# Where the range checks of the inputs run, and which product opens a group of eleven

## The chip, the cores and the metric

The kernel runs on one core of one Trainium2 chip. The metric is the device time of one execution in microseconds, the median of several runs. One execution was also recorded by the hardware profiler; its rows are what is read below. TensorE (PE in the rows, PEld its weight loads), VectorE (DVE), ScalarE (ACT), GpSimd (POOL) and SyncE (SP, which issues most transfers) each work through a queue of their own.

## What is computed

Three layers, one after the other, all in 32-bit floats. The first is a gated linear recurrence over 768 positions, for 2 x 8 heads of width 48; its output, 1536 tokens of 384 features, goes through a feed-forward layer 384 -> 2048 -> 384 with softplus, and that through a mix of four experts 384 -> 1024 -> 384 with relu, weighted by normalised probabilities.

```python
# q, k, v, a_re, a_im: (2, 8, 768, 48); (a_re, a_im) scaled to a length of at most 0.999 first
for t in range(S):
    S_re, S_im = ar * S_re - ai * S_im + k_t v_t^T, ar * S_im + ai * S_re
    y[:, :, t] = q_t @ S_re
x = y.transpose(0, 2, 1, 3).reshape(1536, 384)

h = x @ w_in                                            # 2048 wide
x = (np.maximum(h, 0) + np.log1p(np.exp(-np.abs(h)))) @ w_out

p = domain_probs / (domain_probs.sum(-1, keepdims=True) + 1e-09)
out = sum(p[:, e:e + 1] * (np.maximum(x @ w1[e], 0) @ w2[e]) for e in range(4))   # w1[e] 1024 wide
```

## The kernel before

**Numbers.** Each 32-bit operand is split into a high and a low part (two tiles of one buffer, index 0 and 1), and a product is three matmuls, high by high, low by high and high by low, into the same PSUM tile. A matmul is 128 x 128 weights by 384 columns unless said otherwise.

**Stages.** After the recurrence come twelve stages, run in the order k = 0, 1, 2, 3, 6, 7, 4, 5, 8, 9, 10, 11. k0 and k1 are the two halves of the softplus layer for batch 0, k6 and k7 those for batch 1; k2 to k5 are the four experts for batch 0, k8 to k11 for batch 1. The recurrence of batch 1 is spread over k2 and k3. `base` is the list of the stages' first steps: stage number m of that order begins at `base[m]`, and each has 16 steps (k0 has 24), so `base[3]` is k3, `base[8]` is k8 and `base[12]` the end of k11.

**Plain stages** (k0 to k3, k6, k7): a step is nine matmuls for a first-layer tile `h` (L232, PSUM tag "h", two buffers), the nonlinearity, and, `LAG` = 3 steps later, nine matmuls of the second layer into `y` and `z` (L319). In softplus the nonlinearity is Abs on ScalarE (L247, reads `h`), Exp and Ln on ScalarE (both in L103), then max(h, 0) + that on VectorE (L250, the last reader of `h`), and a split into `g` (L285, L286) a step later.

**Groups of eleven** (the stages in `FAST`, k4, k5 and k8 to k11): two tiles of weights by two blocks of tokens by three slices of the contraction would be 12 products; a scheme of sums and differences makes them from 11, at the price of VectorE and ScalarE work on sums of weights (`sA`, L499, L480, L481) and differences of tokens (`XC`). A group (k, j) is written by `part` in four quarters q = 0 to 3; after each quarter comes the second layer of an earlier tile (nine matmuls). There are four groups to a stage and 24 in all. The group's PSUM tiles are `px` (tag "h", two buffers), `pc` and `pv` (tag "a", three buffers). Quarter 0 of before makes product 7 into `px`, 3 and 4 into `pc`, copies `pc` to `ha` (ScalarE, L437) and adds `px` (VectorE, L438); then product 9 into `pv`, whose value ScalarE copies to `he` (L441). Quarter 1 adds products 0 and 2 to `pv`, so its first matmul must wait until `he` has been copied; the sum is copied to `hb` (L448), product 8 goes onto `px`, and VectorE adds them (L450). Quarter 2 adds two products to `px` and VectorE adds `he` (L456). Quarter 3 adds the last two. Each of the four results is activated (relu into `g`, L425 on ScalarE, L426 on VectorE).

**Range checks.** The fast path holds for inputs within certain ranges. 32 weight checks, `look_w`, each load one 384 KB tile of `w_in` or `w_out` again (`chkw`, L905, issued by SP), take Abs twice on ScalarE into `chkv` (L906, L907) and a maximum on VectorE (L908, `wmax`). Six `look`s at the decays each load two tiles, `chkr` and `chki` (L892, L893), take one Abs on ScalarE (L894) and four operations on VectorE (L895 to L898). All their tiles come from a ring of four buffers with the tag "raw", which the weight loads (`rawA`, `rawB`) use as well. `verdict` (from L911) puts the results together in small VectorE operations, one matmul `fl` (L922) and the flag `bad` (L923). The flag is read at the end of the fast path; where it is set, a general path computes everything anew.

**What sets the order.** `put(units, lo, hi)` spreads pieces of work evenly over the steps from lo to hi; `run` writes everything out in the order of these positions, and a scheduler then orders each engine's queue.

Of the kernel before, what the change touches and what calls it, by code (L numbers as in the profile page):

```python
# [75 lines left out]
def fast_path(ctx: ExitStack, tc, bad, wsc, qkv, a_re, a_im, w_in, w_out, probs, w1, w2, out):  # L76
    nc = tc.nc
# [24 lines left out]
    def act(out_, in_, fn, **kw):  # L102
        i = nc.scalar.activation(out_, in_, fn, **kw)  # L103
        if fn in (AF.Exp, AF.Ln, AF.Sin, AF.Arctan):
# [10 lines left out]
                            base=0, channel_multiplier=-1)  # L115
# [44 lines left out]
    def weights(k, n, tile):  # L160
# [23 lines left out]
        if k >= 2:  # L184
            return [load, lambda: part(z["raw"], slice(0, 768))]
# [9 lines left out]
        def conv(h):  # L195
            sl = slice(h * HW, (h + 1) * HW)
            f = tmp.tile([P, HW], I32, tag="f", name=f"f{nm}_{h}", bufs=2)
            join(nc, f, z["raw"][h])
            part(f.bitcast(F32), sl)
            nc.sync.dma_start(wsc[s * 8 + n, :, sl], f.bitcast(F32))  # L200
# [166 lines left out]
    def halves(b, d, t, q):  # L367
        return XB[b][:, q, d, t * WM:(t + 1) * WM]
# [36 lines left out]
    grp = {}  # L405

    def part(k, j, q):
        b = k // 6
        raws, sums = W[k, 2 * j]

        def prod(ps, w, x, start=False, stop=False):
            lt, li = (raws, w) if w < 5 else (sums, w - 5)
            for n, (p, r) in enumerate(((0, 0), (1, 0), (0, 1))):
                rhs = XC[b][:, r, x, :] if isinstance(x, int) else halves(b, *x, r)
                nc.tensor.matmul(ps, lt[:, p, li, :], rhs, start=(start and n == 0), stop=(stop and n == 2),  # L415
                                 skip_group_check=True)

        def keep(nm):
            return late["u"].tile([P, WM], F32, tag="h", name=f"{nm}{k}_{j}", bufs=3)

        def activate(f, blk, h):
            nm = f"{k}_{blk}_{f}"
            pool = tmp if blk == 0 else late["g"]
            g = pool.tile([P, 2, WM], F32R, tag="g", name="g" + nm, bufs=GB)
            nc.scalar.activation(g[:, 0, :], h, AF.Relu)  # L425
            nc.vector.scalar_tensor_tensor(g[:, 1, :], h, 0.0, g[:, 0, :].bitcast(F32), ALU.max, ALU.subtract)  # L426
            g_t[k, blk, f] = g

        if q == 0:
            x = grp["x"] = psum.tile([P, 512], F32, tag="h", name=f"px{k}_{j}", bufs=2)[:, :WM]  # L430
            c = psum.tile([P, 512], F32, tag="a", name=f"pc{k}_{j}", bufs=3)[:, :WM]
            v = grp["v"] = psum.tile([P, 512], F32, tag="a", name=f"pv{k}_{j}", bufs=3)[:, :WM]
            prod(x, 7, (1, 0), True, True)
            prod(c, 3, 0, True)
            prod(c, 4, (2, 0), False, True)
            h = keep("ha")
            nc.scalar.copy(h, c)  # L437
            nc.vector.tensor_tensor(h, x, h, ALU.add)  # L438
            prod(v, 9, (0, 1), True, True)
            e = grp["e"] = keep("he")  # L440
            nc.scalar.copy(e, v)  # L441
            activate(2 * j + 1, 0, h)
        elif q == 1:
            x, v = grp["x"], grp["v"]
            prod(v, 0, 3)
            prod(v, 2, (2, 0), False, True)
            h = keep("hb")
            nc.scalar.copy(h, v)  # L448
            prod(x, 8, 2, False, True)
            nc.vector.tensor_tensor(h, x, h, ALU.add)  # L450
            activate(2 * j, 0, h)
        elif q == 2:
            x, e = grp["x"], grp["e"]
            prod(x, 2, (2, 1))
            prod(x, 1, 4, False, True)
            nc.vector.tensor_tensor(e, x, e, ALU.add)  # L456
            activate(2 * j, 1, e)
        else:
            x = grp["x"]
            prod(x, 5, (2, 1))  # L460
            prod(x, 6, 1, False, True)
            activate(2 * j + 1, 1, x)
# [287 lines left out]
    def put(units, lo, hi):  # L750
        for i, u in enumerate(units):
            events.append((lo + (hi - lo) * i / len(units), len(events), u))

    def run():
        for _, _, u in sorted(events, key=lambda e: e[:2]):
            u()
        events.clear()
# [32 lines left out]
    base = [0] + [24 + 16 * i for i in range(12)]  # L790
# [96 lines left out]
    def look(part):  # L887
        def run_():
            r, i = (tmp.tile([P, 768], F32, tag="raw", name=f"chk{nm}{part}", bufs=4) for nm in "ri")
            z = hold(f"chkz{part}")  # L890
            rows_ = slice(part * 2 * P, (part + 1) * 2 * P)
            nc.sync.dma_start(r, a_re[rows_, :].rearrange("(p c) j -> p (c j)", p=P))  # L892
            nc.sync.dma_start(i, a_im[rows_, :].rearrange("(p c) j -> p (c j)", p=P))  # L893
            nc.scalar.activation(z, i, AF.Abs)  # L894
            nc.vector.scalar_tensor_tensor(z, r, SLOPE_MAX - 0.01, z, ALU.mult, ALU.subtract)  # L895
            nc.vector.tensor_reduce(vals[:, 0, part:part + 1], r, AX.X, ALU.min)
            nc.vector.tensor_reduce(vals[:, 1, part:part + 1], r, AX.X, ALU.max)
            nc.vector.tensor_reduce(vals[:, 2, part:part + 1], z, AX.X, ALU.min)  # L898
        return run_

    def look_w(i):
        def run_():
            raw = tmp.tile([P, HW, 2], I32, tag="raw", name=f"chkw{i}", bufs=4)
            t = hold(f"chkv{i}")[:, :HW]
            nc.sync.dma_start(raw.rearrange("p a w -> p (a w)"), w_raw[i // 16][i % 16 // 2, i % 2])  # L905
            nc.scalar.activation(t, raw[:, :, 1], AF.Abs)  # L906
            nc.scalar.activation(t, t, AF.Abs, bias=b_mid)  # L907
            nc.vector.tensor_reduce(wmax[:, i:i + 1], t, AX.X, ALU.max)  # L908
        return run_
# [15 lines left out]
    checks = [look_w(i) for i in range(32)]  # L925
    for i in range(6):
        checks.insert(6 * i + 3, look(i))
    put(checks + [verdict], base[8] + 2, base[12] - 2)
    run()
    flush()  # L930

# [153 lines left out]
@with_exitstack  # L1085
def attention_moe_kernel(ctx: ExitStack, tc, qkv, a_re, a_im, w_in, w_out, probs, w1, w2, v, out):
    nc = tc.nc
    top = ctx.enter_context(tc.tile_pool(name="top", bufs=1))
    bad = top.tile([1, 1], I32, name="bad")
    wsc = nc.dram_tensor("moe1_weights", (16, P, 768), F32).ap()  # L1090
    fast_path(tc, bad, wsc, qkv, a_re, a_im, w_in, w_out, probs, w1, w2, out)
    xs = nc.dram_tensor("attention_out", (NTOK, HD), F32).ap()
    flag = nc.values_load(bad[0:1, 0:1], min_val=0, max_val=1)
    with tc.If(flag > 0):
        general_path(tc, xs, v, qkv, a_re, a_im, w_in, w_out, probs, w1, w2, out)
# [53 lines left out]
```

## Time and profile before

| | us |
|---|---|
| median of three runs | 737.11 (736.68 to 737.11) |
| the profiled execution, its own time | 738.36 |
| its span in the profile | 736.6 |
| TensorE matmuls busy | 702.5 |
| TensorE weight loads busy | 674.9 |
| VectorE busy | 586.4 |
| ScalarE busy | 487.4 |
| first matmul of k8, k9, k10, k11 | 527.57, 577.62, 627.22, 673.80 |
| first output transfer issued | 724.13 |

Times of rows are microseconds from the start of the span. The profiled execution is 1.25 us above the median, and 1.76 of its time lie outside its span. Matmuls are pipelined and their recorded ends are modelled, so a stage's price is better read from its length and its number of matmuls than from their busy time. A chain that ended last was not resolved in this profile.

### The profile page before, as it was taken

The numbers are of one execution on the slowest core, as the hardware profiler recorded it, in microseconds if no ns is written. First come the engines' busy times: TensorE is split into PE (matmuls) and PEld (weight loads), VectorE is DVE, ScalarE is ACT, GpSimd is POOL, SyncE is SP. The second block draws the span as 40 slices with busy tenths as digits, with TensorE's granted clock in tenths as the row PEclk, the third lists the DMA queues.
The fourth block names the chain that finished last, engine by engine and source line by source line (L and its number), as shares of the span: only waits on it lengthen the run. The fifth ranks groups of instructions, "written<-read, shape, count | busy, mean of one in ns | idle before, by whom it ended". The sixth has DMA issues, their size and how long they took to land.

```text
span 736.6 us, 13285 instructions
## 1 busy us (share of the span) xinstructions
PE 702.5 (95%) x5159; PEld 674.9 (92%) x5159; DVE 586.4 (80%) x1149; ACT 487.4 (66%) x898; POOL 32.3 (4%) x31
## 2 busy tenths in 40 slices
PE   2789999999999999999999999999999999999996
PEld 1468899999899999999999999999999999999996
DVE  6999999955875854548888779988778898998963
ACT  7887976888896856345686665555556567766640
POOL 1122010000111001000000000000000000000000
PEclk9699999999999999999999999999999999999998
DMA  7665666621211420121022120213445345455401
GB/s 268 195 191 179 201 203 192 224 77 44 86 45 59 122 80 2 59 86 44 23 86 65 43 87 21 87 44 109 119 157 155 127 151 172 150 172 152 162 31 69
DMA packets 36342, 83.56 MB, mean 113 GB/s; under 512 B 4528, under 2 KB 13232, under 8 KB 36272
## 3 DMA queue, kind: packets, MB, share of 16 engines
q1 hardware_dynamic: 36272, 82.64, 35.5%
q8 instruction: 42, 0.69, 0.4%
q14 instruction: 28, 0.23, 0.1%
HBM read 73.95 MB, written 8.65 MB: 112 GB/s over the span
## 4 chain that ended last, share of the span: by engine, by line


## 5 line engine op out<-in xcount | busy, mean ns | idle before, releaser
L232 PE MATMUL h<-X,A 128*128 128x384 f32 (+1 forms) x936 | 175.9, 329 | 2.3 <-ACT A L181 0.8
L232 PEld LDWEIGHTS h<-X,A 128*128 128x128 f32 x936 | 153.4, 188 | 5.6 <-issue 1.6
L319 PE MATMUL y<-B,g 128*128 128x384 f32 x744 | 150.2, 335 | 0.2 <-DVE acc L350 0.2
L319 PEld LDWEIGHTS y<-B,g 128*128 128x128 f32 x744 | 131.0, 188 | 0.7 <-issue 0.5
L319 PE MATMUL y<-g,B 128*128 128x384 f32 (+1 forms) x504 | 91.0, 315 | 0.3 <-ACT g L285 0.3
L319 PE MATMUL z<-B,g 128*128 128x384 f32 x372 | 84.7, 334 | 0.0
L319 PEld LDWEIGHTS y<-g,B 128*128 128x128 f32 x504 | 79.3, 189 | 2.0 <-ACT g L285 0.6
L319 PEld LDWEIGHTS z<-B,g 128*128 128x128 f32 x372 | 66.3, 188 | 0.0
L247 ACT ACTIVATE e<-h 128x384 f32<-128x384 f32 (+1 forms) x60 | 30.8, 512 | 37.1 <-PE h L232 36.0
L250 DVE SCALAR_TENSOR_TENSOR e<-h,e 128x384 f32<-128x384 f32 (+1 forms) x60 | 34.9, 581 | 20.6 <-ACT e L103 19.8
L255 DVE SCALAR_TENSOR_TENSOR g<-h,g 128x384 fp32r<-128x384 f32 x32 | 17.7, 555 | 28.1 <-ACT g L254 28.1
L103 ACT ACTIVATE e<-e,b_one 128x384 f32<-128x384 f32 (+1 forms) x60 | 38.2, 637 | 1.3
L103 ACT ACTIVATE e<-e 128x384 f32<-128x384 f32 (+1 forms) x60 | 32.8, 547 | 1.3
L415 PE MATMUL px<-X,sA 128*128 128x384 f32 x144 | 33.4, 340 | 0.0
L319 PE MATMUL z<-g,B 128*128 128x384 f32 x144 | 32.9, 335 | 0.0
L415 PE MATMUL px<-XC,sA 128*128 128x384 f32 x144 | 32.8, 336 | 0.0
L664 PE MATMUL tp<-ident,QK 128*96 128x128 f32 x192 | 27.2, 288 | 5.7 <-DVE QK L655 4.6
L664 PEld LDWEIGHTS tp<-ident,QK 128*96 128x96 f32 x192 | 22.2, 133 | 10.3 <-DVE QK L655 6.2
L254 ACT ACTIVATE g<-h 128x384 fp32r<-128x384 f32 x32 | 15.6, 488 | 21.3 <-PE h L232 21.1
L286 DVE TENSOR_TENSOR g<-e,g 128x384 fp32r<-128x384 f32 x48 | 26.6, 555 | 3.7 <-ACT g L285 2.9
L480 ACT CAST B<-rawB 128x768 fp32r<-128x768 f32 x24 | 20.0, 834 | 14.4 <-DMA rawB<-in_w_dram 7.3
L350 DVE SCALAR_TENSOR_TENSOR acc<-y,pr,acc 128x384 f32<-128x384 f32 x46 | 26.3, 612 | 1.7 <-PE y L319 1.7
(204 smaller groups left out, 1416.7 us busy)
## 6 DMA issues: line engine op xcount, KB each, us to landing
rawA<-in_w_dram SPq DMA_DIRECT2D x32, 384.0 KB, 3.0
rawB<-in_w_dram SPq DMA_DIRECT2D x32, 384.0 KB, 3.1
rawA<-in_w_in_dram SPq DMA_DIRECT2D x16, 384.0 KB, 3.5
rawB<-in_w_out_dram SPq DMA_DIRECT2D x16, 384.0 KB, 3.8
chkw<-in_w_in_dram SPq DMA_DIRECT2D x16, 384.0 KB, 3.2
chkw<-in_w_out_dram SPq DMA_DIRECT2D x16, 384.0 KB, 3.2
qk<-in_qkv_dram SPq DMA_DIRECT2D x12, 384.0 KB, 3.4
v<-in_qkv_dram SPq DMA_DIRECT2D x12, 256.0 KB, 2.9
```

The lines of the kernel that those rows point to most:

```text
L103: i = nc.scalar.activation(out_, in_, fn, **kw)
L232: nc.tensor.matmul(ps, wt[:, p, kk, o:o + P], XB[b][:, q, kk, tok], start=(n == 0), stop=(n == 3 * KT - 1))
L247: nc.scalar.activation(t, h, AF.Abs)
L250: nc.vector.scalar_tensor_tensor(t, h, 0.0, t, ALU.max, ALU.add)
L254: nc.scalar.activation(g[:, 0, :], h, AF.Relu)
L255: nc.vector.scalar_tensor_tensor(g[:, 1, :], h, 0.0, g[:, 0, :].bitcast(F32), ALU.max, ALU.subtract)
L286: nc.vector.tensor_tensor(g[:, 1, :], t, g[:, 0, :].bitcast(F32), ALU.subtract)
L319: mm = nc.tensor.matmul(ys[j], l_, r_, start=(opens and n == 0 and not mate), stop=(closes and n == 2), skip_group_check=k == 0)
L350: nc.vector.scalar_tensor_tensor(dst, ys[j], pcol, dst, ALU.mult, ALU.add)
L415: nc.tensor.matmul(ps, lt[:, p, li, :], rhs, start=(start and n == 0), stop=(stop and n == 2), skip_group_check=True)
L480: nc.scalar.copy(hi, src)
L664: nc.tensor.transpose(tp[:96, hh, :], src[:, hf * 4 + hh, :], ident)
```

## The change

The 38 checks keep their sequence and are spread over the steps from `base[3] + 2` (in k3) to `base[8] - 2` (the end of k5) instead of `base[8] + 2` to `base[12] - 2`; the verdict alone stays behind, over the last two steps but one. In quarter 0 of each group product 9 into `pv` and the copy `he` are written first, then `px`, `pc` and `ha`. What an operation does is the same, and so is the number of operations. In the kernel after, the copy `he` is L435, the copy `ha` L440 and its sum L441.

```diff
@@ -430,15 +430,15 @@
             x = grp["x"] = psum.tile([P, 512], F32, tag="h", name=f"px{k}_{j}", bufs=2)[:, :WM]
             c = psum.tile([P, 512], F32, tag="a", name=f"pc{k}_{j}", bufs=3)[:, :WM]
             v = grp["v"] = psum.tile([P, 512], F32, tag="a", name=f"pv{k}_{j}", bufs=3)[:, :WM]
+            prod(v, 9, (0, 1), True, True)
+            e = grp["e"] = keep("he")
+            nc.scalar.copy(e, v)
             prod(x, 7, (1, 0), True, True)
             prod(c, 3, 0, True)
             prod(c, 4, (2, 0), False, True)
             h = keep("ha")
             nc.scalar.copy(h, c)
             nc.vector.tensor_tensor(h, x, h, ALU.add)
-            prod(v, 9, (0, 1), True, True)
-            e = grp["e"] = keep("he")
-            nc.scalar.copy(e, v)
             activate(2 * j + 1, 0, h)
         elif q == 1:
             x, v = grp["x"], grp["v"]
@@ -925,7 +925,8 @@
     checks = [look_w(i) for i in range(32)]
     for i in range(6):
         checks.insert(6 * i + 3, look(i))
-    put(checks + [verdict], base[8] + 2, base[12] - 2)
+    put(checks, base[3] + 2, base[8] - 2)
+    put([verdict], base[12] - 2, base[12] - 1)
     run()
     flush()
 
```

**TensorE, the fourth group of k8.** Names carry the stage and the group or tile, so `px8_3` belongs to group 3 of k8; the last number only tells buffers apart. X1 holds batch 1's tokens, XC1 their differences. The queue before:

```order
L319 MATMUL z8_1_0_6291<-B8_1_5929,g8_1_3_6242 128x384 x3
L415 MATMUL px8_3_6398<-X1_2458,sA8_3_6302 128x384 x3
L415 MATMUL pc8_3_6399<-XC1_5174,A8_3_6100 128x384 x3
L415 MATMUL pc8_3_6399<-X1_2458,A8_3_6100 128x384 x3
L415 MATMUL pv8_3_6400<-X1_2458,sA8_3_6302 128x384 x3
L319 MATMUL y8_0_4_6421<-B8_2_6103,g8_0_4_6324 128x384 x6
L319 MATMUL z8_0_4_6422<-B8_2_6103,g8_0_4_6324 128x384 x3
L415 MATMUL pv8_3_6400<-XC1_5174,A8_3_6100 128x384 x3
```

and after:

```order
L319 MATMUL z8_1_0_6509<-B8_1_6181,g8_1_3_6466 128x384 x3
L415 MATMUL pv8_3_6606<-X1_2458,sA8_3_6520 128x384 x3
L415 MATMUL px8_3_6604<-X1_2458,sA8_3_6520 128x384 x3
L415 MATMUL pc8_3_6605<-XC1_5346,A8_3_6346 128x384 x3
L415 MATMUL pc8_3_6605<-X1_2458,A8_3_6346 128x384 x3
L319 MATMUL y8_0_4_6627<-B8_2_6349,g8_0_4_6542 128x384 x6
L319 MATMUL z8_0_4_6628<-B8_2_6349,g8_0_4_6542 128x384 x3
L415 MATMUL pv8_3_6606<-XC1_5346,A8_3_6346 128x384 x3
```

The first product into `pv8_3` moved from behind `pc8_3` to the front of the quarter; between it and the next product into `pv8_3` now stand 18 matmuls, where there were nine.

**ScalarE, the same group.** Before, with a weight check among the copies:

```order
L425 ACTIVATE g8_1_5_6371<-px8_2_6261 128x384
L480 CAST sA9_0_6433<-mA9_0_6432 128x640
L480 CAST B9_1_6464<-rawB9_1_6462 128x768
L906 ACTIVATE chkv7_6494<-chkw7_6493 128x384
L437 COPY ha8_3_6410<-pc8_3_6399 128x384
L907 ACTIVATE chkv7_6494<-chkv7_6494,b_mid_106 128x384
L441 COPY he8_3_6416<-pv8_3_6400 128x384
L425 ACTIVATE g8_0_7_6418<-ha8_3_6410 128x384
L480 CAST A9_2_6516<-rawA9_2_6514 128x384
L448 COPY hb8_3_6453<-pv8_3_6400 128x384
```

and after:

```order
L425 ACTIVATE g8_1_5_6583<-px8_2_6485 128x384
L480 CAST sA9_0_6639<-mA9_0_6638 128x640
L480 CAST A9_3_6826<-rawA9_3_6824 128x384
L480 CAST A9_3_6826<-rawA9_3_6824 128x256
L435 COPY he8_3_6610<-pv8_3_6606 128x384
L440 COPY ha8_3_6621<-pc8_3_6605 128x384
L425 ACTIVATE g8_0_7_6624<-ha8_3_6621 128x384
L448 COPY hb8_3_6653<-pv8_3_6606 128x384
```

The check's two operations are gone from here, and `he8_3` is copied ahead of `ha8_3`.

**ScalarE, the second and third softplus steps of k7.** Three operations a step (Abs, Exp, Ln). Before:

```order
L247 ACTIVATE e7_0_1_4498<-h7_0_1_4488 128x384
L103 ACTIVATE e7_0_1_4498<-e7_0_1_4498 128x384
L103 ACTIVATE e7_0_1_4498<-e7_0_1_4498,b_one_102 128x384
L247 ACTIVATE e7_0_2_4534<-h7_0_2_4524 128x384
L103 ACTIVATE e7_0_2_4534<-e7_0_2_4534 128x384
L103 ACTIVATE e7_0_2_4534<-e7_0_2_4534,b_one_102 128x384
L480 CAST sA4_1_5013<-mA4_1_5012 128x640
L480 CAST A4_0_4704<-rawA4_0_4702 128x384
L480 CAST A4_0_4704<-rawA4_0_4702 128x256
L247 ACTIVATE e7_0_3_4564<-h7_0_3_4554 128x384
```

and after:

```order
L247 ACTIVATE e7_0_1_4606<-h7_0_1_4596 128x384
L906 ACTIVATE chkv13_4663<-chkw13_4662 128x384
L103 ACTIVATE e7_0_1_4606<-e7_0_1_4606 128x384
L907 ACTIVATE chkv13_4663<-chkv13_4663,b_mid_106 128x384
L103 ACTIVATE e7_0_1_4606<-e7_0_1_4606,b_one_102 128x384
L247 ACTIVATE e7_0_2_4642<-h7_0_2_4632 128x384
L906 ACTIVATE chkv14_4725<-chkw14_4724 128x384
L103 ACTIVATE e7_0_2_4642<-e7_0_2_4642 128x384
L907 ACTIVATE chkv14_4725<-chkv14_4725,b_mid_106 128x384
L103 ACTIVATE e7_0_2_4642<-e7_0_2_4642,b_one_102 128x384
```

Weight checks 13 and 14 now stand between the Abs, the Exp and the Ln of these steps, and the conversion of weights `A4_0` behind them has moved to another place.

## Rows read from the trace of the kernel before

**Rows 1.** The page, part 1: busy us of each engine, share of the span, instructions.

```profile
PE 702.5 (95%) x5159; PEld 674.9 (92%) x5159; DVE 586.4 (80%) x1149; ACT 487.4 (66%) x898; POOL 32.3 (4%) x31
```

**Rows 2.** Busy time by stage: us, engines (instructions), granted clock, DMA share, GB/s.

```profile
253.73:382.03 128.30, 128.30 (x1109) 124.77 (x1108) 84.66 (x151) 72.99 (x129) 4.60 (x4) 1.00 0.18 55
382.03:432.94 50.91, 50.91 (x292) 50.91 (x291) 42.30 (x100) 35.28 (x70) 0.00 (x0) 1.00 0.20 63
432.94:527.57 94.63, 94.63 (x547) 94.42 (x546) 82.26 (x179) 53.40 (x107) 0.00 (x0) 1.00 0.22 68
527.57:577.62 50.05, 49.56 (x278) 47.85 (x277) 42.05 (x88) 28.05 (x56) 0.00 (x0) 1.00 0.49 151
577.62:627.22 49.60, 49.13 (x278) 47.97 (x277) 44.45 (x91) 32.16 (x64) 0.00 (x0) 1.00 0.48 157
627.22:673.80 46.58, 46.58 (x269) 46.58 (x268) 43.20 (x88) 29.96 (x58) 0.00 (x0) 1.00 0.53 164
673.80:723.76 49.96, 49.96 (x289) 49.68 (x288) 38.22 (x84) 27.33 (x54) 0.00 (x0) 1.00 0.29 93
```

**Rows 3.** Waits of the weight loads, k8 and k9: total us, times, longest.

```profile
PEld pv L415 <- ACT he L441: 1.8, 4, 0.7
PEld px L415 <- DVE hb L450: 0.6, 2, 0.4
PEld y L319 <- issue: 0.5, 1, 0.5
PEld px L415 <- DVE he L456: 0.4, 2, 0.2
PEld y L319 <- DVE g L426: 0.3, 1, 0.3
```

**Rows 4.** The same view for k10 and k11, up to the last product.

```profile
PEld fl L922 <- issue: 0.2, 1, 0.2
```

**Rows 5.** Timeline of ScalarE in k8: start, us, instruction, [idle before <-releaser].

```profile
566.55 0.55 ACT L906 ACTIVATE chkv<-chkw 128x384 f32<-128x384 int32 x1 [1.36 <-DMA chkw<-in_w_in_dram]
...
567.88 0.47 ACT L441 COPY he<-pv 128x384 f32<-128x384 f32 x1
```

**Rows 6.** Timeline of TensorE at the same place.

```profile
565.73 0.69 PE L415 MATMUL pv<-X,sA 128*128 128x384 f32 x3
...
568.40 0.79 PE L415 MATMUL pv<-XC,A 128*128 128x384 f32 x3 [0.42 <-ACT he L441]
```

**Rows 7.** Weight checks: count, ns min/median/max, first and last start; idle until.

```profile
L906 ACT ACTIVATE chkv<-chkw x32: 536/553/567, 512.3 to 705.9; 128x384 f32<-128x384 int32 x32
L907 ACT ACTIVATE chkv<-chkv,b_mid x32: 600/617/624, 512.9 to 706.5; 128x384 f32<-128x384 f32 x32
L908 DVE TENSOR_REDUCE wmax<-chkv x32: 542/553/556, 513.6 to 707.1; 128x1 f32<-128x384 f32 x32
...
  DMA chkw<-in_w_in_dram: 6.3, 7
```

**Rows 8.** Looks at the decays: two of their five operations, same columns.

```profile
L894 ACT ACTIVATE chkz<-chki x6: 829/847/852, 538.4 to 689.5; 128x768 f32<-128x768 f32 x6
...
L895 DVE SCALAR_TENSOR_TENSOR chkz<-chkr,chkz x6: 947/950/958, 543.5 to 690.7; 128x768 f32<-128x768 f32 x6
```

**Rows 9.** Timeline in k7, one softplus step: TensorE (twice), ScalarE, VectorE.

```profile
388.30 1.75 PE L232 MATMUL h<-X,A 128*128 128x384 f32 x9
...
394.62 1.75 PE L232 MATMUL h<-X,A 128*128 128x384 f32 x9
...
390.09 0.50 ACT L247 ACTIVATE e<-h 128x384 f32<-128x384 f32 x1 [1.41 <-PE h L232]
...
392.18 0.55 DVE L250 SCALAR_TENSOR_TENSOR e<-h,e 128x384 f32<-128x384 f32 x1
```

**Rows 10.** Timeline of the end: VectorE's flag, the output transfers of SP.

```profile
715.38 0.15 DVE L923 TENSOR_SCALAR bad<-fl 1x1 int32<-1x1 f32 x1
...
724.13 7.06 SPq L352 DMA_DIRECT2D out_dram<-acc  x6
```

## The prediction

> **What bounds the kernel now.** I read the page's busy shares first: TensorE's matmuls are busy 95% of the span, its weight loads 92%, VectorE 80%, ScalarE 66% [rows 1]. TensorE is the engine to fill, and the change takes no matmul from it, so all that can be won is time in which it stands still, and all that can be lost is new standstill.
>
> Second, the table by stage [rows 2]; the stages follow one another as k3 and k6 (first row), k7, k4 and k5, k8, k9, k10, k11. Dividing each row's length by its matmuls gives the price of one: 128.30/1109 holds other matmul sizes and is left aside; k7 has 50.91/292 = 174 ns; k4 and k5, 94.63/547 = 173.0; k10, 46.58/269 = 173.2; k11, 49.96/289 = 172.9; but k8, 50.05/278 = 180.0, and k9, 49.60/278 = 178.4. The granted clock is 1.00 in all of them. So only k8 and k9 lose time, although the checks run in k8 to k11 alike and k10 has the busiest VectorE of the four (43.20 of 46.58 us, 93%).
>
> Third, the waits of the weight loads in k8 and k9 [rows 3]: 1.8 us in four waits of `pv` for the ScalarE copy `he` (L441), 0.6 for `hb`, 0.4 for VectorE's `he`, 0.5 that names no releaser and 0.3 for `g`, 3.6 in sum. In k10 and k11 there is 0.2, before the one matmul of the verdict [rows 4].
>
> Fourth, one of those waits close up. ScalarE stood 1.36 us for a check's transfer at 566.55, and behind that check came the copy `ha`, the check's second step, and only at 567.88 the copy `he` [rows 5]. TensorE had put the first product into `pv` at 565.73, ending at 566.42; the next product into `pv`, due when nine matmuls of the second layer were through, began at 568.40 with 0.42 us idle recorded [rows 6]. A check that waits for memory holds up a copy on which TensorE depends.
>
> As a rule beside that, the Trainium skill ("PSUM — Partial Sum Buffer", Engine vs sequencer instructions) says that ScalarE and VectorE queues are strictly first in, first out; the trace agrees at 566.55.
>
> **What goes away.** k8: 278 x (180.0 - 173.2) = 1.9 us. k9: 278 x (178.4 - 173.2) = 1.4 us. With the 0.2 of k11, 3.5 us; the waits give 3.6 + 0.2 = 3.8, and since part of a wait is absorbed by the matmuls in flight I take the smaller, rounded to 3.4. Both halves of the change work on it. The checks leave these stages with 32 x (0.553 + 0.617) + 6 x 0.85 = 42.5 us of ScalarE work and 32 x 0.553 + 6 x 4 x 0.95 = 40.5 of VectorE work [rows 7, 8] (the 0.95 of L895 taken for each of a look's four steps, an estimate, as all run over the same tile). With `he` copied first, nine matmuls more (9 x 173 = 1.56 us) lie between the product into `pv` and the next one, so the copy has 3.1 us where it had 1.56, and `ha` no longer stands ahead of it.
>
> The Trainium skill ("Perfetto Trace Analysis", Identifying the Most-Contended Engine) holds matmul busy time a poor measure of TensorE and weight-load busy time a better one. By matmul busy [rows 2] k8 and k9 would yield only 0.49 + 0.47 = 1.0 us, by weight-load busy 2.20 + 1.63 = 3.8; the trace's price per matmul, 3.3, sides with the page.
>
> **What it costs ahead of k8.** The 38 checks now lie between about the start of k3 and the end of k5: 527.57 - 253.73 = 274 us instead of about 195 (512.3 to 707.1 [rows 7]), so they come less densely, one in 7.2 us instead of one in 5.1. By the order in which they stand on ScalarE: 8 weight checks up to the end of k3, 5 in k6, 9 in k7, 10 in k4 and k5; of the six looks one, two, one and two. TensorE is full in all these stages; nothing in the trace of before shows a check beside softplus work, so I bound the cost from both sides.
>
> Lower end, 0: k3 and k6 have room (VectorE 84.66 of 128.30 us, ScalarE 72.99). In k7 the chain of one softplus step is the tight spot: the product `h` ends at 390.05, Abs starts at 390.09, VectorE reads the bank until 392.73, and the same bank (two in rotation) is written again at 394.62 [rows 9]: 1.9 us of slack. A check's pair between those steps, as the new order has it, takes 0.553 + 0.617 = 1.17 and leaves 0.7. A gain from these moves I exclude there: no row of these stages has standstill to give back.
>
> Upper end: the price k8 and k9 paid. Of the 38 checks about half (100 us of 195) ran in them for 3.3 us, 0.17 us a check; 38 x 0.17 = 6.6 us. What speaks for it is load. k7: VectorE 42.30 + 8 x 0.553 + 3.8 = 50.5 of 50.91 us, ScalarE 35.28 + 9 x 1.17 + 0.85 = 46.7. k4 and k5: VectorE 82.26 + 11 x 0.553 + 2 x 3.8 = 95.9 of 94.63, 101%; the sums count neighbouring operations that overlap at their edges in full, so 97 to 100% is nearer, and weight conversions that the checks push along can run some microseconds late, being ahead of need. ScalarE there is light, 53.40 + 10 x 1.17 + 1.7 = 66.8 of 94.63.
>
> Middle value: before, the four stages lost 3.4 us to 38 checks, 0.09 each. Half of that was the wait for `he` (1.8 of 3.6), which the new sequence takes out in k4 and k5 too; that leaves 38 x 0.045 = 1.7 us. k10 is the nearest row (93% VectorE load, no standstill) and would say 0; the load of 97 to 100% says more. I take 1.8.
>
> **Edits with one answer.** The verdict's matmul now stands 24 matmuls further on, 24 x 0.173 = 4.2 us, so the flag falls at 715.38 + 4.2 = 719.6, before the output transfers that start at 724.13 [rows 10]: nothing, and were that cover gone the tail would move by the excess. The transfers move ahead of two batches of attention and weight loads on SP; the loads have room while DMA is busy 0.18 to 0.22 of the time [rows 2], and later, at 0.5, they get the room back. The sum `ha` comes 0.5 us later, and its result is used three quarters of a group further on: nothing.
>
> **The sum.** The profiled run took 738.36 us, 1.25 above the median of 737.11. -3.4 + 1.8 = -1.6: the profiled run would come to 736.8, the median to 735.5.
>
> **The rivals.** (a) The checks vanish under the stages ahead: 737.1 - 3.4 = 733.7. For it k10 without a stall and the lower density; against it VectorE near 100% in k7 and k5. (b) The stalls only move: 0.09 each at the new place as at the old, 737.1; for it that the transfers, two or three of four buffers and the in-order queue come along; against it the reordered `pv`. (c) Slower: a check whose transfer is late holds ScalarE's queue, and now what stands behind it is the Exp and the Ln of a softplus step in k6 and k7 and the copies `he` and `hb` in k4 and k5; with the price that k8 and k9 paid for late transfers, 0.17 a check, the time is 737.1 - 3.4 + 6.6 = 740.3. It decides from where the wait for the transfer exceeds the 0.7 us left in the chain; of the 32 weight checks seven waited for a transfer of `w_in`, on average 6.3/7 = 0.9 us [rows 7], so some would exceed it, and those in the emptier k3 and k6 would not. If ScalarE could run on past a waiting check, (c) would fall and (a) be left; by the skill's queue rule above it cannot. (d) The change doesn't do what it says, because the emission order holds the checks back to the last stages: 737.1. Against it stands the order, in which ScalarE meets weight checks 13 and 14 inside k7.
>
> **How the numbers follow.** A measurement of this kernel can tell about 0.2%, 1.47 us: faster is below 735.64, slower above 738.58. Forecast (1.0 to 2.2 of new stalls, 734.7 to 735.9) 0.35; (a) and what lies between it and the forecast 0.25; (b) and what lies between 735.9 and 738.6 0.23; (c) 0.15; (d) 0.02. Of the forecast's 0.35 some 0.08 lies above 735.64. Faster 0.27 + 0.25 = 0.52, same 0.08 + 0.23 + 0.02 = 0.33, slower 0.15. The range, 733.4 to 738.9, reaches from just under (a) to where (c) begins and leaves most of (c) out. For the likeliest alone it is 734.7 to 735.9.
>
> **What would show it.** Right: in the profile after, k8 and k9 near 173 ns a matmul like k10, and no wait of `pv` for a copy in any stage; k7, k4 and k5 between 173 and 176, with waits for `hb`, `he` of VectorE or for the softplus chain. Wrong: k8 and k9 still at 178 or more (then neither checks nor copies were the cause); k7 at 177 or more with `h` waiting for VectorE (rival c, softplus), or k5 there with `px` waiting for `hb` (rival c, VectorE full); k7, k4 and k5 all at 173 (rival a).

## The result, and the profile after

The changed kernel takes 741.87 us (median of 12 runs, 738.98 to 745.74), the kernel before 737.38 us in 12 runs of the same session. The ratio is 1.0062, with a 95% interval of 1.0049 to 1.0075: slower by 4.5 us. The forecast was 735.5.

The stages, as in [rows 2]; k3 and k6 together, then k7, k4, k5, k8, k9, k10. The columns are the stretch, its length, the busy time of TensorE, its weight loads, VectorE, ScalarE and GpSimd (with instructions), the granted clock, the DMA share and GB/s.

```profile
253.90:384.30 130.40, 129.35 (x1109) 124.63 (x1108) 97.15 (x171) 84.78 (x152) 4.00 (x4) 1.00 0.35 106
...
384.30:435.50 51.20, 51.14 (x292) 50.82 (x291) 47.95 (x109) 42.94 (x87) 0.00 (x0) 1.00 0.43 132
435.50:483.60 48.10, 47.01 (x269) 46.28 (x269) 45.19 (x96) 30.36 (x63) 0.00 (x0) 1.00 0.39 118
483.60:535.10 51.50, 49.53 (x280) 47.96 (x279) 47.76 (x109) 32.36 (x67) 0.00 (x0) 1.00 0.43 132
535.10:583.40 48.30, 48.30 (x278) 48.11 (x278) 38.24 (x87) 24.13 (x47) 0.00 (x0) 1.00 0.35 110
583.40:631.60 48.20, 48.20 (x278) 48.02 (x277) 35.95 (x77) 22.78 (x44) 0.00 (x0) 1.00 0.22 66
631.60:679.90 48.30, 48.30 (x278) 48.12 (x278) 36.05 (x77) 22.78 (x44) 0.00 (x0) 1.00 0.19 59
```

The price of a matmul in k8 and k9 fell as forecast, from 180.0 and 178.4 to 48.30/278 = 173.7 and 48.20/278 = 173.4 ns: 278 x (6.3 + 5.0) = 3.1 us won. But k3 and k6 grew from 128.30 to 130.40 (+2.1), k7 from 50.91 to 51.20 (+0.3), and k4 and k5 from 94.63 to 48.10 + 51.50 = 99.60 (+5.0; that the counts of matmuls differ by two is a matter of the stretches' edges). Added up, +7.4 - 3.1 = +4.3 us; the spans differ by 740.8 - 736.6 = 4.2.

The waits of the weight loads in k4 and k5, where there were none [rows 2] (total us, times, longest):

```profile
PEld px L415 <- DVE hb L450: 2.6, 3, 1.4
PEld px L415 <- DVE he L456: 2.1, 3, 1.7
PEld ns L396 <- DVE zr L394: 0.2, 1, 0.2
PEld y L319 <- DVE g L426: 0.2, 1, 0.2
PEld px L415 <- DVE ha L441: 0.2, 1, 0.2
```

No wait of `pv` for the copy `he` is left, in any stage: the new sequence did what it says. What k4 and k5 have now is six waits of `px` for VectorE's two sums, `hb` and `he`, 4.7 us together, and two of them make up 3.1. The largest, in k5, first on ScalarE, then VectorE, then TensorE (start, us, instruction, [idle before <-releaser]):

```profile
517.01 0.55 ACT L906 ACTIVATE chkv<-chkw 128x384 f32<-128x384 int32 x1 [1.71 <-DMA chkw<-in_w_out_dram]
517.46 0.51 ACT L389 ACTIVATE nz<-X 128x384 f32<-128x384 f32 x1
517.87 0.60 ACT L907 ACTIVATE chkv<-chkv,b_mid 128x384 f32<-128x384 f32 x1
...
518.80 0.51 ACT L425 ACTIVATE g<-hb 128x384 fp32r<-128x384 f32 x1
...
518.51 0.55 DVE L908 TENSOR_REDUCE wmax<-chkv 128x1 f32<-128x384 f32 x1 [1.84 <-ACT chkv L907]
...
519.44 0.55 DVE L426 SCALAR_TENSOR_TENSOR g<-hb,g 128x384 fp32r<-128x384 f32 x1
519.91 0.55 DVE L456 TENSOR_TENSOR he<-px,he 128x384 f32<-128x384 f32 x1
...
518.58 0.51 PE L319 MATMUL y<-B,g 128*128 128x384 f32 x2
520.52 0.80 PE L415 MATMUL px<-X,sA 128*128 128x384 f32 x3 [1.43 <-DVE he L456]
```

ScalarE waits 1.71 us for a check's transfer; VectorE, whose next instruction is that check's maximum, waits 1.84 us for ScalarE; the sum `he` stands behind the maximum, and behind a `g` (L426) whose first half ScalarE made at 518.80, after the check; TensorE waits for the sum. One late transfer, handed on through three queues. That transfer, issued at 512.29, landed 4.7 us later and is the slowest of the 32:

```profile
DMA to landing us min/median/max: 2.9/3.3/4.7
```

With the middle duration it would have landed at about 515.6 (an estimate, 512.29 + 3.3), and ScalarE was free at 515.3.

The other large wait, 1.4 us in k4, has the same shape:

```profile
440.06 0.55 ACT L906 ACTIVATE chkv<-chkw 128x384 f32<-128x384 int32 x1 [0.58 <-DMA chkw<-in_w_out_dram]
...
441.06 0.56 DVE L426 SCALAR_TENSOR_TENSOR g<-ha,g 128x384 fp32r<-128x384 f32 x1 [0.60 <-ACT g L425]
441.57 0.55 DVE L908 TENSOR_REDUCE wmax<-chkv 128x1 f32<-128x384 f32 x1
...
442.91 0.55 DVE L450 TENSOR_TENSOR hb<-px,hb 128x384 f32<-128x384 f32 x1
...
443.51 0.79 PE L415 MATMUL px<-X,A 128*128 128x384 f32 x3 [1.09 <-DVE hb L450]
```

Over the whole kernel, the idle time before the weight checks' operations (us, times), until:

```profile
  ACT chkv L907: 11.2, 11
  DMA chkw<-in_w_out_dram: 5.1, 7
  DMA chkw<-in_w_in_dram: 5.0, 4
```

Before, ScalarE waited 10.7 us for these transfers and VectorE 4.3 us for L907; now 10.1 and 11.2. These totals don't measure the loss: 6.2 of the 11.2 us lie in k3 and only 3.2 in k4 and k5, and the largest part of ScalarE's waits in one stage, 3.8 us, lies in k6, which lost 0.3.

In k3 the recurrence of batch 1 is what is held up. These are three of the waits of the weight loads there, and none of them is in that stage before:

```profile
PEld tp L664 <- ACT qT L665: 0.8, 1, 0.8
...
PEld yps L689 <- DVE A L674: 0.6, 1, 0.6
PEld pl L578 <- DVE hl L575: 0.5, 1, 0.5
```

Before the sum `hl` of the third, VectorE stood 0.95 us for ScalarE's part of a look at the decays and then did its own part (L895, 0.96 us). What made the other two late was not followed back.

### The profile page after: what moved, and what is told of

Same layout as the page of the kernel before. It is cut to its first block, busy times and chain, and to the rows that moved or that the text cites. A ratio compares the mean times of both kernels' runs of the same rounds, so it can differ in the third digit from the quotient of the medians.

```text
span 740.8 us, 13329 instructions
## 1 busy us (share of the span) xinstructions
PE 704.8 (95%) x5159; PEld 675.4 (91%) x5159; DVE 584.0 (79%) x1149; ACT 485.6 (66%) x898; POOL 33.1 (4%) x31
## 4 chain that ended last, share of the span: by engine, by line
## 5 line engine op out<-in xcount | busy, mean ns | idle before, releaser
L481 DVE TENSOR_TENSOR B<-rawB,B 128x768 fp32r<-128x768 f32 x24 | 23.0, 957 | 6.8 <-ACT B L480 6.8
L415 PEld LDWEIGHTS px<-X,sA 128*128 128x128 f32 x144 | 25.2, 188 | 2.8 <-DVE he L456 2.1
```

What stands on the lines that cost most here:

```text
L481: nc.vector.tensor_tensor(lo, src, hi.bitcast(F32), ALU.subtract)
```

## The experiments

Ratios are to the kernel before, run in the same session, with 95% intervals.

**Each half alone.** First the new sequence with the checks at their old place, then the new place with the old sequence.

```diff
-    put(checks, base[3] + 2, base[8] - 2)
-    put([verdict], base[12] - 2, base[12] - 1)
+    put(checks + [verdict], base[8] + 2, base[12] - 2)
```

> The second half of the change alone: product 9 and the copy he come first, the checks stay in k8 to k11. Theory (the loss comes from late check transfers and VectorE's full queue in k4 and k5, and the new sequence is good): the waits of pv for he, 1.8 us in k8 and k9, go; those for hb and he of VectorE (1.5 us) stay; 735.5 to 736.3, ratio 0.998. Rival (the new sequence itself costs, since pc and the copy ha come 0.5 us later and VectorE's sum with them): 737.4 or more, with new waits of px or y.

Measured: 737.31 us against 738.13, ratio 0.9983 (0.9971 to 0.9996). k8 and k9 take 48.80 us each for 278 matmuls, 175.5 ns, where they took 180.0 and 178.4:

```profile
527.80:576.60 48.80, 48.80 (x278) 47.80 (x277) 41.63 (x87) 28.29 (x56) 0.00 (x0) 1.00 0.49 154
576.60:625.40 48.80, 48.61 (x278) 47.98 (x277) 43.83 (x92) 32.42 (x64) 0.00 (x0) 1.00 0.50 162
```

The waits of `pv` for `he` are gone and 1.3 us of `px` for VectorE's sums are left. The sequence is good by itself, and this kernel is the fastest of all that keep the checks.

> The first half alone: the checks move ahead of k8, quarter 0 stays as it was. Theory: k8 to k11 run at 174 ns a matmul, k3 to k5 lose what the changed kernel lost there (7.4 us) and the waits of pv for he besides, 1 to 2 us: 742.5 to 744. Rival (the sequence costs): 737 to 740, with k4 and k5 near 175 ns a matmul.

```diff
-    put(checks + [verdict], base[8] + 2, base[12] - 2)
+    put(checks, base[3] + 2, base[8] - 2)
+    put([verdict], base[12] - 2, base[12] - 1)
```

Measured: 739.99 us, ratio 1.0020 (1.0007 to 1.0033). The new place costs by itself, but less than with the new sequence (1.0062), against my expectation. k3 and k6 lose as much (130.30 us); k4 and k5 take 47.40 and 48.90 us for 269 and 280 matmuls, 175.4 ns, instead of 181.4. VectorE's wait for a check's result in k4 and k5, the changed kernel's row ahead of this one's:

```profile
DVE wmax L908 <- ACT chkv L907: 3.2, 3, 1.8
```

```profile
DVE wmax L908 <- ACT chkv L907: 0.2, 1, 0.2
```

The transfers were less late here, too: in k4 and k5 ScalarE waited 2.1 us for them, at most 0.7 at a time, and in the changed kernel 4.0, at most 1.7. So the difference goes with how late the transfers are and how VectorE stands behind them, not with the checks' number or place. It doesn't go with VectorE's load either, which in k5 is that of the changed kernel (47.76 us in 109 operations):

```profile
483.30:532.20 48.90, 48.90 (x280) 47.99 (x279) 47.49 (x109) 33.31 (x69) 0.00 (x0) 1.00 0.46 145
```

What makes the lateness differ between the two sequences is taken up below (transfers ahead).

**Without the checks.** Both kernels without them set the results to constants at the head of the program.

```diff
+    nc.gpsimd.memset(vals, 1.0)
+    nc.gpsimd.memset(wmax, 0.0)
...
-    put(checks, base[3] + 2, base[8] - 2)
```

> The changed kernel without the 38 checks (their results are set to constants that let the fast path stand; the range checks are left out, the rest is computed). Theory: no stage loses anything to checks, k3 72.6 us, k4 to k11 at 173 to 175 ns a matmul: 733.5 to 734.5. Rival (sequence costs): k4 and k5 still above 178 ns, 736 or more.

> The kernel before without the 38 checks (set to constants as in the other). Theory: without a check nothing on ScalarE is late for he, so the sequence is worth nothing: as the kernel without checks in the new sequence within 0.5 us, 733.5 to 734.5. Rival (VectorE's and ScalarE's own load makes the waits, not the checks): waits of pv for he remain, 735 to 736.

Measured: ratios 1.0053 (1.0033 to 1.0074) and 1.0053 (1.0029 to 1.0078), slower than with the checks. The loss is at the other end of the kernel: k0 took 93.10 and 91.10 us instead of 85.00, at a granted clock of 0.95 and 0.96 there instead of 1.00. The two constants had changed the order in which the first stages' operations stand in their queues, so the totals say nothing of the checks. In k8 and k9 both run at 48.20 to 48.30 us, the old sequence too: without checks there is no wait of `pv` to remove. The repair was to set the constants by VectorE, from data that exist only after k1.

> The changed kernel without the 38 checks, as before, but with the constants set by VectorE from tokens of batch 0, so that nothing of it stands in the queues at the start (the range checks are left out). If the first kernel without checks lost its 9 us in k0 by its constants alone: k0 near 84 us, k3 72.6, k4 to k11 at 173.5 to 175, ratio to before 0.994 to 0.997. Rival (the missing checks themselves disturb the start): k0 again above 90 us, ratio above 1.004.

Measured: 735.71 us against 737.54, ratio 0.9975 (0.9963 to 0.9987). k0 84.90 us, k3 and k6 128.40, k7, k4 and k5 50.90, 46.30 and 48.30: every stage at its full rate. That is the floor, some 1.8 us below before: the whole price of the checks at their old place, and all that any placing of them could win.

**Load or transfer?** The prediction had VectorE at 97 to 100% in k7, k4 and k5. This run keeps the load and takes the transfers and their buffers away.

```diff
-            nc.sync.dma_start(raw.rearrange("p a w -> p (a w)"), w_raw[i // 16][i % 16 // 2, i % 2])
+            raw = XB[0][:, 0, 0, :].bitcast(I32).rearrange("p (a w) -> p a w", w=2)
...
-            nc.vector.tensor_reduce(wmax[:, i:i + 1], t, AX.X, ALU.max)
+            nc.vector.tensor_reduce(junk[:, 3:4], t, AX.X, ALU.max)
```

> The changed kernel with every operation of the checks on ScalarE and VectorE at its place, but none of their 44 transfers and none of the buffers for them: the operations read tokens of batch 0 instead, and their results are dropped (the range checks are left out). Theory one (late transfers, passed on through the queues of ScalarE and VectorE): k3 falls from 74.5 to 72.6 us, k4 and k5 from 180 and 186 to under 176 ns a matmul; within 1.5 us of the kernel without checks. Rival (the load alone: VectorE has 97 to 100% to do in k7 to k5): k3, k4 and k5 stay as in the changed kernel, ratio to before 1.004 to 1.007.

Measured: 736.99 us, ratio 0.9987 (0.9973 to 1.0001). k7, k4 and k5:

```profile
383.20:433.90 50.70, 50.70 (x292) 50.53 (x291) 48.03 (x113) 43.94 (x93) 0.00 (x0) 1.00 0.20 64
433.90:480.40 46.50, 46.50 (x269) 46.27 (x269) 45.49 (x98) 32.42 (x66) 0.00 (x0) 1.00 0.19 59
480.40:528.70 48.30, 48.30 (x280) 48.20 (x279) 43.33 (x98) 28.68 (x58) 0.00 (x0) 1.00 0.24 82
```

In k4 VectorE is busy 45.49 of 46.50 us, 98%, more than the 45.19 of 48.10 in the changed kernel, and TensorE loses nothing; in k7 48.03 of 50.70. The load alone isn't it. Some of the operations now run earlier than in the changed kernel (k5 has fewer of them), so for k5 this run is weaker evidence than for k7 and k4; there the new place with the old sequence, 97% busy and 0.6 us lost, speaks against the load. k3 falls to 73.4 us, from 74.4, against 72.6 without checks: some 0.8 of its 1.8 us is the operations themselves.

**Without VectorE's part.** Transfers and ScalarE's operations stay, L895 to L898 and L908 go.

> The changed kernel with the checks' transfers and ScalarE operations, without their VectorE operations (the range checks are left out). Theory one (late transfers): half of the loss in k4 and k5 stays, since the copies ha, hb and he still stand behind a late check on ScalarE, k4 and k5 together 2 us or more above the kernel without checks; k3 as in the changed kernel or near it. Rival (VectorE's load): k4 and k5 at 174 ns, within 1 us of the kernel without checks.

Measured: ratio 1.0029 (1.0013 to 1.0046). k7 and k5 run at their full rate or nearly (50.90 us; 48.50 for 280 matmuls, 173.2 ns); k4 takes 48.90 us, 2.5 more than before. In k4 there is a loss, then, that needs no VectorE operation of a check: ScalarE waited 2.1 us for the checks' transfers there, and TensorE's weight loads 1.0 us for the copy `he` and 1.1 for VectorE's `hb`. k5 decides nothing, because the transfers were hardly late in it any more: ScalarE waited 0.3 us for them, where it had waited 2.3.

**Fewer buffers.** Results over inputs: one buffer of four for a weight check instead of two.

```diff
...
-            t = hold(f"chkv{i}")[:, :HW]
+            t = raw[:, :, 0].bitcast(F32)
```

> The changed kernel with the checks' results written over their inputs, so that a weight check takes one buffer of the ring of four instead of two, and a look two instead of three; nothing else changes. Theory one, with the ring as the reason why transfers are late: ScalarE's waits for a check's transfer fall under 5 us in all (10.1 in the changed kernel), k4 and k5 lose 2 us or less instead of 5, ratio to before 1.000 to 1.003. Rival (load alone, or transfers late for another reason): ratio 1.005 to 1.007.

Measured: 743.50 us, ratio 1.0077 (1.0050 to 1.0104). ScalarE waited 9.4 us for the weight checks' transfers, no less than the 10.1. My reason for the lateness, that the checks wait for buffers of their own making, fell.

**Transfers ahead.** In four kernels, the two sequences at the two places, transfers and operations became pieces of their own, the former one and a half steps ahead, and the results were written over the inputs as in the run above.

```diff
...
-    put(checks, base[3] + 2, base[8] - 2)
+    put([c[0] for c in checks], base[3] + 2 - 1.5, base[8] - 2 - 1.5)
+    put([c[1] for c in checks], base[3] + 2, base[8] - 2)
```

> The changed kernel with the checks' transfers issued one and a half steps (some 4.5 us) ahead of their operations, and the results written over the inputs so that the ring of four holds them. Theory one (a transfer that has only just been issued holds ScalarE's queue, then VectorE's, then TensorE): ScalarE's waits for a check's transfer fall below 3 us in all, k4 and k5 under 176 ns a matmul, k3 at 73.5; ratio to before 0.997 to 1.000, against 1.0077 for the kernel with results in place alone. Rival (the transfers themselves are in the way, as traffic or by the buffers they hold, whenever they are issued): ratio 1.004 or more, and waits of the weight conversions for their loads.

> The new sequence alone, checks in k8 to k11, with the transfers one and a half steps ahead and results in place. Theory one: k8 to k11 all at 174 to 175.5 ns a matmul, 1 us less than the new sequence alone: ratio 0.996 to 0.998. Rival (transfers in the way): as the new sequence alone or worse, 0.9983 to 1.003.

> The new place alone, old sequence, with the transfers ahead and results in place. The new place without the new sequence was better (1.0020) than with it (1.0062). Theory one (how far a check's transfer is late when ScalarE comes to it is what differs between them): with the transfers ahead the two sequences lie within 0.15% of each other. Rival (the new sequence itself hurts in k4 and k5): this one is 0.3% better than the new place with the new sequence and early transfers.

> The kernel before with the transfers ahead and results in place, nothing else. Theory one: the waits of pv for he in k8 and k9 (1.8 us) go with the late transfers, k8 and k9 at 176 or less; ratio 0.996 to 0.998. Rival (it is the order on ScalarE, he behind ha and the check's own 1.17 us): 1.8 us of waits of pv stay, ratio 0.999 to 1.001.

Measured: 1.0087 (1.0055 to 1.0120), 1.0033 (1.0020 to 1.0046), 1.0089 (1.0063 to 1.0114) and 1.0052 (1.0027 to 1.0077), in this order. The last three are worse than the same kernels without the edit (0.9983, 1.0020 and 1); the first can't be told from the changed kernel (1.0062), nor from the one with only the results in place (1.0077), and what that part of the edit cost in the others isn't separated. And the edit didn't do what it was meant to. It seems that the scheduler puts a check's operation into ScalarE's queue where it reckons the transfer done, whatever step it is written in: the middle distance from the issue of a transfer to its operation was 3.7 and 3.5 us in the first two, 4.0 in the changed kernel and 3.7 before. ScalarE's waits for the weight checks' transfers grew instead of falling, from 10.1 to 14.0 us in the changed kernel, from 5.4 to 18.1 in the sequence alone and from 7.8 to 14.7 in the place alone. The changed kernel with transfers ahead, who waited for `chkw` (us, times), and the transfers' time:

```profile
  ACT chkw L916: 14.0, 18
...
DMA to landing us min/median/max: 2.9/3.3/5.4
```

So this is no test of early transfers; in the first three it is one of more waits, and in the second and third the loss grew with them. In the fourth the waits stayed (9.7 us, 10.7 before), and `pv` still waited 1.4 us for `he`; its profiled run is the fastest of its five, and what its ratio rests on isn't explained. The comparison of the first and the third bears on the question left by the two halves: with their checks in nearly the same places, new and old sequence cost the same at the new place, 1.0087 and 1.0089, though intervals of 0.3% to either side don't exclude the 0.4% by which the old one was better without this edit. Those 0.4% fit a chance meeting of checks and transfers, like the single transfer of 4.7 us in k5, and no property of the sequence; that isn't shown.

**Transfers that nobody reads.** All transfers and buffers stay, and the operations read batch 0's tokens.

> The changed kernel with all 44 transfers and their buffers, but the checks' operations read tokens of batch 0 instead of what was loaded, so that no engine waits for a transfer of a check (the range checks are left out). Without transfers the loss was gone (0.9987). Theory one (ScalarE's and VectorE's queues stand behind a transfer that is just under way): gone here too, k4 and k5 under 175.5 ns a matmul, ratio 0.997 to 1.000. Rival (the transfers as traffic, or as users of the ring that make the weights late): k4 and k5 at 178 or more, ratio 1.003 to 1.007.

Measured: 744.79 us, ratio 1.0075 (1.0050 to 1.0100). The run didn't separate what it should: the results still went into the ring's buffers, so ScalarE's operations waited 6.8 us for transfers that lay in the buffer before, and VectorE 7.1 us for them. So the results were moved into a tile of their own.

```diff
+    scratch = const.tile([P, WM], BF16, name="scratch")
...
-            t = hold(f"chkv{i}")[:, :HW]
+            t = scratch
```

> The changed kernel with all 44 transfers into their buffers of the ring, none of which is read, and with the checks' operations on tokens of batch 0 and into a tile outside the ring; free of the transfers, those operations now run early, all of them in k2, k3 and k6 (the range checks are left out). In k7, k4 and k5 the transfers are alone. Theory one (engines lose by standing behind a transfer under way): k7, k4 and k5 at 175.5 ns a matmul or less, as without transfers. Rival (the transfers as traffic or as users of the ring delay the weights): k4 and k5 at 178 or more, with waits for the weights' loads and conversions.

Measured: 739.35 us, ratio 1.0019 (1.0002 to 1.0036). Of k7, k4 and k5, which now hold transfers alone, two are at full rate and one isn't:

```profile
384.70:435.20 50.50, 50.50 (x292) 50.50 (x291) 43.16 (x102) 36.52 (x73) 0.00 (x0) 1.00 0.50 151
435.20:483.60 48.40, 47.51 (x269) 46.16 (x269) 42.30 (x91) 25.92 (x53) 0.00 (x0) 1.00 0.43 131
483.60:531.90 48.30, 48.30 (x280) 48.09 (x279) 40.06 (x90) 25.13 (x50) 0.00 (x0) 1.00 0.35 115
```

In k5 the 3.2 us are gone: there the transfers as traffic cost nothing. The checks' operations have left k5 as well, so this run alone doesn't tell their load from their standing behind a transfer; the new place with the old sequence does, as said above. In k4 2.0 us are left, and the largest wait there (0.9 us of the weight loads) follows a weight that came late, on ScalarE, VectorE and TensorE in turn:

```profile
446.61 0.82 ACT L482 CAST A<-rawA 128x384 fp32r<-128x384 f32 x2 [2.16 <-DMA rawA<-in_w_dram]
...
450.82 0.55 DVE L443 TENSOR_TENSOR ha<-px,ha 128x384 f32<-128x384 f32 x1
...
451.43 0.79 PE L417 MATMUL px<-XC,sA 128*128 128x384 f32 x3 [0.61 <-DVE ha L443]
```

So each theory came true in one stage: k5 lost nothing once no operation stood behind a check's transfer, and in k4 a weight was late beside the transfers alone. That the second goes by the ring of four buffers and SP's queue is argued: SP's weight loads waited 23.8 us for checks' transfers in k7, k4 and k5 (10 times), but the way to this one weight wasn't followed.

**Another queue for the transfers.** GpSimd issues them instead of SP.

> The changed kernel with the checks' 44 transfers issued by GpSimd's queue instead of SP's, so that a check's transfer that waits for a buffer no longer holds up the weight loads behind it on SP, nor a weight load the check. If SP's queue makes the transfers late: ScalarE's waits for them under 5 us (10.1 in the changed kernel), ratio 1.000 to 1.003. If it is the ring or the just-in-time order itself: waits and ratio as in the changed kernel, 1.005 to 1.008.

Measured: 747.78 us, ratio 1.0133 (1.0104 to 1.0162). ScalarE waited 15.0 us for the weight checks' transfers in 15 waits. SP's order alone isn't the reason for the lateness; freed from it, the waits grew.

**Another engine for the operations.** The weight checks on GpSimd, in seven short operations, at both places.

```diff
-            nc.scalar.activation(t, raw[:, :, 1], AF.Abs)
-            nc.scalar.activation(t, t, AF.Abs, bias=b_mid)
-            nc.vector.tensor_reduce(wmax[:, i:i + 1], t, AX.X, ALU.max)
+            nc.gpsimd.tensor_scalar(t, raw[:, :, 1], 2.0 ** -30, None, ALU.mult)
+            nc.gpsimd.tensor_tensor(t, t, t, ALU.mult)
...
```

> The changed kernel with the 32 weight checks computed on GpSimd, which has nothing else to do there (seven short operations each, counting the values outside the window; the results stay in place), so that GpSimd and not ScalarE waits for their transfers; the six looks stay where they were. Theory one: the weight checks cost nothing, the looks a little; k4 and k5 under 176 ns, k3 under 73.5, ratio 0.997 to 1.000. Rival (traffic and ring): 1.003 or more. A third possibility is GpSimd too slow or in VectorE's way: its operations above 1.5 us each, or VectorE's own operations longer than before.

> The new sequence with the weight checks in k8 to k11 on GpSimd in the same way. Theory one: faster than the new sequence alone (0.9983), ratio 0.9965 to 0.998, with k8 to k11 at 174 to 175.5 ns. Rival (traffic and ring): no better than 0.9983; GpSimd too slow for 195 us: worse than 1.000.

Measured: 1.1965 (1.1920 to 1.2009) and 1.1883 (1.1840 to 1.1925). Only what I had set down as a further possibility, GpSimd too slow or in VectorE's way, comes near this. From the first of the two kernels, two of the seven operations (ns min/median/max, first and last start), then two of ScalarE's waits from k3 to k5:

```profile
L908 POOL TENSOR_SCALAR chkw<-chkw x32: 1205/1228/3151, 251.4 to 656.1; 128x384 f32<-128x384 int32 x32
L909 POOL TENSOR_TENSOR chkw<-chkw x32: 825/827/1396, 252.9 to 657.4; 128x384 f32<-128x384 f32 x32
```

```profile
ACT B L482 <- DMA rawB<-in_w_dram: 28.3, 5, 11.2
...
ACT A L482 <- DMA rawA<-in_w_dram: 20.3, 6, 8.1
```

A check now holds its buffer through some 7 us of operations, one after the other, and the weights, which need the same four buffers, come up to 11.2 us late. The ring, held too long, is not all of it: one of VectorE's sums (the second half of the softplus `g`) took 0.62 us on average and up to 1.08, in the changed kernel 0.56 and never over 0.57, and TensorE, which stood still often, had a granted clock of 0.88 in k3 and 0.80 in k7 instead of 1.00. The shares aren't separated, and the question of an idle engine waiting for transfers stays untried.

## Why the prediction was wrong

**What goes away** was right in its mechanism, and in its size from profile to profile: 3.4 us forecast, 3.1 measured in k8 and k9, and no wait of `pv` for a copy left. The sequence alone confirms its half (2.1 us in k8 and k9). In many runs it is less: the kernel without checks is 1.8 us (1.0 to 2.7) faster than before, so the 3.4 us that I read from one profiled execution, 1.25 us above the median, were too many.

**What it costs ahead of k8** was the step that failed, and by its middle value: 1.8 us forecast, 7.4 measured from profile to profile, above the upper end of 6.6 that I had taken from k8 and k9. By the ratios of many runs, 1.0062 with the checks and 0.9975 without, it is 0.0087 x 737 = 6.4 us (some 5 to 8), so near that end. Three sentences of it carried the error.

The first took k10 for the nearest row and halved the price of a check because the waits for the copy `he` would go. They went; but a late transfer holds more than that copy. VectorE waits for the check as well, and the sums `hb` and `he` stand behind it, where no new sequence helps. The row that says so was in the trace of before: the waits for `hb` and `he` in [rows 3], 1.0 of 3.6 us. I carried them over at that size with the half that stayed, and in k4 and k5 they came to 4.7 us.

The second was "k3 and k6 have room". Their VectorE was busy 66% of the time [rows 2], but k3 holds the recurrence, a chain in which each step waits for the one before; 2.1 us were lost there. Busy shares say nothing of a chain's slack. The run without transfers shows that some 0.8 us of it come from the operations alone.

The third was the load of VectorE. I counted it for the upper end, and the run without transfers shows 98% in k4 with nothing lost, the new place with the old sequence 97% in k5 with 0.6 us lost. The size was near, and the reason was wrong.

**The rivals.** (c) came closest: 740.3, against 741.87, a late transfer as the mechanism, and the rate of k8 and k9 for all 38 checks. I gave it 0.15, and the range ended at 738.9, where it began. Its place was half wrong: k7 with its softplus chain lost 0.3 us; k3 and k6, which it left out, lost 2.1; and in k4 and k5 TensorE waited for VectorE's sums, not for ScalarE's copies. So part of its nearness is luck. The sign that I had named for k5, `px` waiting for `hb`, came, but I had given VectorE's load as its reason. (a), 733.7, was below what even the kernel without checks reaches (0.9975 of before, about 735.3).

**The rule of the queues**, strictly first in, first out (the Trainium skill, "PSUM — Partial Sum Buffer", Engine vs sequencer instructions), agrees with the chain at 517.01, and it should have been followed one engine further: ScalarE's queue held VectorE's.

**What stays open.** Why the transfers are late where they are late: it was neither the results' buffers alone (in place, 9.4 us of waits) nor SP's queue alone (GpSimd's, 15.0), and why the one in k5 took 4.7 us isn't known. Half of the weight checks start within 4.0 us of their transfer's issue, and a transfer took 2.9 to 4.7 us in the changed kernel, so the operation is queued for about the moment of landing; a kernel that truly queues it later wasn't made. In k4 1.1 us of TensorE's standstill follow a check, as shown above; how the rest of its loss divides between late checks and late weights isn't shown, and neither is the way in which k3 loses the 1.0 us that aren't the operations.

## What to carry to other kernels

Optional work with a transfer of its own isn't free because the engines have gaps: where its operation is queued for the moment of landing, a late landing can be handed on through every in-order queue that the result passes, and what decided here was who stood behind it, not how busy the engine was. Ahead of moving such work, look in the stage it goes to for what is next in each of those queues, and for chains, whose slack a busy share doesn't show. A copy on which the busiest engine depends belongs as early in its group as it can stand; that part is worth keeping here, at 0.9983, with the checks where they were.

## What the runs showed of the hardware

A VectorE that was busy 98% of a stage didn't hold up TensorE there (k4 without transfers). The same kind of transfer, 384 KB, took 2.9 to 4.7 us from issue to landing within one execution of the changed kernel. GpSimd took 1.23 us for an operation with a scalar on 128 x 384 values and 0.83 us for one with two tensors, where VectorE's maximum over as many took 0.55; in the kernel with GpSimd at work, one of VectorE's sums, 0.55 to 0.57 us in the changed kernel, took up to 1.08.
